# Gram products in rounds of four, logits copied by ScalarE, turned gate factors and four system transfers in a delta-attention and mixture-of-experts kernel

## The chip, the cores and the metric

The kernel runs as one program on one core of a Trainium2 chip. The metric is the device time of one execution in microseconds (us); lower is better. Five engines work side by side, each through its own list of instructions in order: TensorE (PE; its weight loads are listed as PEld), VectorE (DVE), ScalarE (ACT), GpSimd (POOL) and SyncE (SP), which here only issues DMA transfers. ACT and POOL issue some transfers too.

## The reference

All of it is in float32. Three stages follow each other: a delta-rule attention over 4 x 8 heads with a state of 48 x 48 per head, a dense layer with a squared ReLU, and a top-1 mixture of eight experts.

```python
# q, k, v: (4, 8, 768, 48); beta: (4, 8, 768)
k_n = k / (np.linalg.norm(k, axis=-1, keepdims=True) + 1e-06)
for t in range(S):
    y[:, :, t] = np.einsum('bhd,bhde->bhe', q[:, :, t], state)
    v_old = np.einsum('bhde,bhd->bhe', state, kt)
    state = state + bt[:, :, :, None] * np.einsum('bhd,bhe->bhde', kt, vt - v_old)
x = y.transpose(0, 2, 1, 3).reshape(3072, 384)
x = np.maximum(x @ w_in, 0.0) ** 2 @ w_out            # w_in (384, 2048)
logits = x @ w_gate                                    # w_gate (384, 8)
gate_w = softmax(logits)[argmax]                       # one factor per token
out[token] = gate_w * (np.maximum(x @ w1[e], 0) @ w2[e])   # e = argmax, w1 (8, 384, 1024)
```

## The kernel before

**Chunks and units.** The 768 steps of the attention are cut into 12 chunks of 64. For each chunk the dense layer is computed in 8 units: `l1_unit` (18 products `h`, L682) and, two units later, `l2_unit` (12 products `x`, L710). The attention of later chunks is spread between these units as generators. A chunk has 16 half-unit slots, and the tables `PRE2_AT` and `CHAIN_AT` say at which slot a generator makes its next step (`step_bg`). Every engine runs what it gets in this order.

**Preparing a chunk: `pre(c)`.** For c from 4 on it starts two chunks ahead. `front(c)` turns keys and queries on DVE (`kq`, L381, from the loaded tile `st`), and then makes the Gram products of the keys with keys and queries: 32 heads, in four groups (`grams`, L383 to L409) at slots 5, 6, 7 and 8. A group takes 4 times two products `gm` (L392 and L393), each of 48 rows by 64 columns of weights and 128 columns of data, into one PSUM bank. Each product is two passes in the trace, so that a group is 16 records. ACT empties the bank: `gd` (keys with keys), and `kq` for the queries, which POOL then masks (L401). `bounce` writes `gd` to a buffer `dg` in device memory (4 transfers from ACT, slot 8); `bounced` reads it back as `gl`, with one small system in each partition (2 transfers from SP, slot 8.6).

**Solving: `solve`.** From slot 12.3 on DVE solves 64 triangular systems of 32 x 32 per chunk, 31 steps of a product (`tmp`, L520) and a subtraction (`pt`, L525). The first instruction is a square root on ACT (L476) of the diagonal of `gl`. At the end SP writes the result to `dt` (2 transfers, L535) and reads it back in another order as `tt` (8 transfers, L545). `gl` has one buffer, so that the next one can't be loaded before the solve has read the last.

**The chain: `chain(c)`**, in the chunk before c: at slot 7 it loads `ktok` and multiplies `z` (L583); then `u` from `tt` and `vz` (L594, slot 10.6), `z`, `u`, and `y` twice, which make the dense layer's input `xt`; the state is updated by `ku` (L641) at slot 0.1 of the next chunk. All of these small products, the transposes and the logits take turns in four PSUM banks of the pool `ps_a`: the n-th tile gets the bank of the (n-4)-th, and waits until that one is read.

**Routing: `route(c)`**, in the chunk after c: the output rows of the dense layer are written to device memory (`xs_d`, L727), transposed (`xp`, L734) and multiplied by the gate weights (`lp`, L742); DVE copies the logits to `lga` (L743), and finds the expert and the place in its list, which POOL scatters to `list_d` (L793). `gates` (L799) turns the logits into gate factors, and SP writes them to `g_d` token by token: for 10 chunks 4 transfers of 64 x 10 single floats from `ga` (L809).

**Experts.** From the last chunk on: `load_ids` reads a list (SP, L1017), `gather` fetches the rows `xg` from `xs_d` and `gather_gate` the factors `gg` from `g_d` (POOL, L1023 and L1032), `transposed` turns the rows on PE (`xp`, L1045), and `slot` does two products per expert (`h` L1059, `y` L1071). Slots 0 and 1 have 256 rows; slots 2 to 9 up to 384 (L1081, L1091). The weights are loaded as `raw` (SP, 7 transfers of 384 or 512 KB per slot) and split by ACT and DVE into `ew`.

Of the kernel before, what the change touches and what calls it, by code (L numbers as in the profile page):

```python
# [41 lines left out]
def kernel(  # L42
# [19 lines left out]
    P = 128  # L62
# [302 lines left out]
    def front(c):  # L365
# [20 lines left out]
        def grams(hf, g, c0, c1):  # L386
# [9 lines left out]
            for x in range(2):  # L396
# [10 lines left out]
                if c0 == 0 and c1 == P:  # L407
                    nc.scalar.copy(kq[l, x, rs, 32:64], gm[l, :, 32:64])

        masks = []  # L410

# [5 lines left out]
        def bounce():  # L417
            dgv = dg.rearrange("(u r two) s t -> u two s r t", u=2, two=2)
# [28 lines left out]
        else:  # L447
            yield
            transposes(1)
            load_v(c)  # L450
            yield
            for n, hg in enumerate(groups):
                masked()
                grams(*hg, 0, P)
                if n == 3:
                    bounce()
                yield
# [10 lines left out]
    def solve(cs):  # L468
# [28 lines left out]
        def norms(n):  # L497
            c = cs[n]
            nps = ps_a.tile([P, NPR], F32, tag="a", name="nps")
            for x in range(2):  # L500
                for hf in range(2):
                    for u in range(2):
                        r0, l0 = quad(x, hf), 32 * u + 16 * hf
                        nc.tensor.matmul(nps[r0:r0 + 32, HP * u:HP * u + HP], nl[0:64, part[n]], ident[0:64, l0 + x:l0 + 16:2], start=True, stop=True)
# [32 lines left out]
        for c, dt in zip(cs, dts):  # L537
            tt = ap_.tile([P, 2, HP, 32], F32, tag="tt", bufs=2, name=f"tt{c}")
            tt_t[c] = tt
            dtr = dt.rearrange("(u f r two) j t -> f two u j r t", u=2, f=2, two=2)  # L540
            for u in range(2):
                for hf in range(2):
                    for x in range(2):
                        r0 = quad(x, hf)
                        (nc.gpsimd if c == 0 and x else nc.sync).dma_start(out=tt[r0:r0 + 32, u], in_=dtr[hf, x, u])  # L545
            yield
# [14 lines left out]
    def chain(c):  # L561
# [4 lines left out]
        if c + 1 < NCH:  # L566
            ktok = ap_.tile([P, NPR, D], F32, tag="ktok", name=f"ktok{c}")
            load_k(c, ktok)
        if c == 0:
            yield  # L570
# [18 lines left out]
        def u_step(u):  # L589
            ut = ps_a.tile([P, HP, D], F32, tag="a", name="u")  # L590
            for j in range(HP):
                for hf, x in heads:
                    o = quad(x, hf)
                    nc.tensor.matmul(ut[o:o + 32, j], tt[o:o + 32, u, j], vt[o:o + 32, u, j], start=True, stop=True)  # L594
            for hf, x in heads:
# [121 lines left out]
    def route(c):  # L717
# [81 lines left out]
    def gates(c0, c1):  # L799
# [3 lines left out]
        nc.scalar.activation(lf, lf, AF.Exp)  # L803
        nc.vector.tensor_reduce(out=ga, in_=lf, axis=AX.X, op=ALU.add)
        nc.vector.tensor_scalar(ga, ga, 1e-9, None, op0=ALU.add)
        nc.vector.reciprocal(ga, ga)
        gv = ga.rearrange("p (c t) -> p t c", t=2)
# [17 lines left out]
    def load_bl():  # L825
        for par in range(2):
            for u in range(2):
                r0 = 64 * par + 32 * u
                nc.gpsimd.dma_start(out=bl[r0:r0 + 32], in_=bf[:, :, u, :])

# [335 lines left out]
    for n, (c, i) in enumerate(units):  # L1166
# [32 lines left out]
        if c == NCH - 1 and i == 0:  # L1199
            gates(0, NCH - 2)  # L1200
        if c == NCH - 1 and i == 2:
            for n in range(NFS):
                gx[n] = gather(n, ids[n]) + (gather_gate(n, ids[n]),)
        if c == NCH - 1 and i > NF // 2 - 1 - KD:
# [4 lines left out]
    for a in pend:  # L1209
        l2_unit(*a)  # L1210
        split_w(0, j)
        j += 1
    xT_next, todo = transposed(0)
    for t in todo:
        t()
    last = route(NCH - 1)
    advance(last)
    while j < NW:
        split_w(0, j)
        j += 1  # L1220
    tab = slot_table()

    def ahead(s):
# [4 lines left out]
    def slot(s):  # L1228
# [21 lines left out]
        for i in range(NF2 // 2):  # L1250
# [9 lines left out]
            split_w(s + 1, 2 * i)  # L1260
            if s == 0:
                if i == 2:
                    run(last)
                    gates(NCH - 2, NCH)
                    ahead(0)
            turn_one()
# [113 lines left out]
```

## Time and profile before

| | |
|---|---|
| median of 3 runs | 1021.74 us (1018.74 to 1023.69) |
| the profiled execution: its time, its span | 1019.3 us, 1017.5 us |
| busy in the span: PE, DVE, ACT, POOL | 910.4, 664.9, 514.3, 315.4 us |
| mean granted clock of TensorE, as a share of full speed | 0.957 |
| Gram products `gm`: records, first to last | 768, 10.9 to 601.8 us |

The time is 1.8 us longer than the span, from the first to the last instruction in the trace. All later times are counted from the start of the span. The attention with the dense layer goes on until about 711 us, the experts until the end. An engine's busy time says how long something ran on it, not that it set the end; that is read from the waits in each stretch.

### The profile page before, as it was taken

What the parts mean: (1) busy time and instruction counts of PE and PEld (TensorE: products, weight loads), DVE (VectorE), ACT (ScalarE), POOL (GpSimd) and SP (SyncE); (2) the same over time, 40 slices, a digit from 0 to 9 for tenths busy, and PEclk for the clock granted to TensorE, in tenths of its full rate; (3) what the DMA queues carried; (4) which work ended last, traced back from release to release, by engine and by line L of the source; (5) the groups of instructions that cost most, each with busy time, mean ns of one, the idle gap of its engine ahead of it and who ended that gap; (6) DMA issues with size and microseconds to landing.
All of it is one profiled execution on the core that took longest, in us unless ns stands there. A gap on an engine that the chain in (4) does not pass through costs nothing.

```text
span 1017.5 us, 28821 instructions
## 1 busy us (share of the span) xinstructions
PE 910.4 (89%) x11416; PEld 849.9 (84%) x11416; DVE 664.9 (65%) x2270; ACT 514.3 (51%) x1025; POOL 315.4 (31%) x322
## 2 busy tenths in 40 slices
PE   6267979999899999999999999999789999999995
PEld 5135868988898888888888988999779999998994
DVE  6987897584949495868686777424564554463653
ACT  5146755555354645454545555455444444464553
POOL 2020023333142424242424342210434334353231
PEclk9689889999899999999999999999899999999998
DMA  8899292535343443435342531218786555564764
GB/s 159 139 184 272 40 103 31 84 38 85 49 83 50 77 56 57 61 57 74 63 72 49 80 55 38 38 55 140 139 251 209 158 165 174 165 218 136 236 199 133
DMA packets 273021, 113.82 MB, mean 112 GB/s; under 512 B 241053, under 2 KB 259554, under 8 KB 272096
## 3 DMA queue, kind: packets, MB, share of 16 engines
q1 hardware_dynamic: 244176, 92.87, 43.3%
q0 software_dynamic: 7344, 15.17, 5.8%
q10 hardware_dynamic: 21344, 3.67, 2.2%
q8 instruction: 100, 1.64, 0.8%
q14 instruction: 57, 0.47, 0.2%
HBM read 95.01 MB, written 17.82 MB: 111 GB/s over the span
## 4 chain that ended last, share of the span: by engine, by line
PE 54%; DVE 18%; DMA 12%; issue 5%; SPq 5%; ACT 4%; POOL 1%; another core or an unknown queue 0%; ACTq 0%; DVEq 0%; POOLq 0%
PE h L682 12%; PE x L710 11%; PE h L1059 6%; PE y L1071 5%; DVE tmp L520 5%; DVE pt L525 4%; PE h L1081 4%; PE y L1091 3%; DVE kq L381 2%; DMA raw<-in_moe_w_dram 2%; PE gm L392 2%; DMA xs_d<-xr 2%; PE wa L1091 2%; DMA st<-in_q_dram 1%; DMA xg<-xs_d,ids 1%
## 5 line engine op out<-in xcount | busy, mean ns | idle before, releaser
L682 PE MATMUL h<-xt,win 128*128 128x256 f32 x1728 | 235.1, 291 | 6.0 <-issue 2.9
L710 PE MATMUL x<-wout,gt 128*128 128x384 f32 x1152 | 229.1, 347 | 2.7 <-issue 2.3
L682 PEld LDWEIGHTS h<-xt,win 128*128 128x128 f32 x1728 | 220.6, 195 | 12.4 <-issue 5.1
L710 PEld LDWEIGHTS x<-wout,gt 128*128 128x128 f32 x1152 | 200.9, 192 | 9.7 <-issue 6.9
L692 POOL TENSOR_TENSOR gt<-r,gt 128x512 fp32r<-128x512 f32 x80 | 103.7, 1296 | 320.5 <-ACT gt L688 216.5
L520 DVE TENSOR_TENSOR tmp<-pt,gl 128x60 f32<-128x60 f32 (+37 forms) x662 | 142.4, 254 | 1.8
L686 ACT ACTIVATE r<-h 128x512 f32<-128x512 f32 x96 | 57.4, 597 | 166.9 <-PE h L682 118.9
L525 DVE TENSOR_TENSOR pt<-pt,tmp 128x60 f32<-128x60 f32 (+37 forms) x662 | 135.1, 243 | 4.3 <-remote 3.0
L973 DVE TENSOR_TENSOR ew<-raw,ew 128x768 fp32r<-128x768 f32 (+1 forms) x98 | 102.3, 1069 | 9.2 <-ACT ew L972 8.5
L1059 PE MATMUL h<-xgT,ew 128*128 128x256 f32 x648 | 85.0, 287 | 7.5 <-issue 4.5
L1059 PEld LDWEIGHTS h<-xgT,ew 128*128 128x128 f32 x648 | 82.1, 195 | 9.8 <-issue 7.3
L972 ACT CAST ew<-raw 128x768 fp32r<-128x768 f32 (+1 forms) x98 | 87.4, 923 | 1.9 <-DMA raw<-in_moe_w_dram 1.9
L1071 PE MATMUL y<-ew,ht 128*128 128x384 f32 x432 | 86.3, 347 | 0.0
L1071 PEld LDWEIGHTS y<-ew,ht 128*128 128x128 f32 x432 | 75.7, 193 | 0.1
L1101 POOL DMA_INDIRECT out_dram<-yo,ids x30 | 30.2, 1005 | 127.3 <-ACT yo L1100 119.2
L1063 DVE SCALAR_TENSOR_TENSOR ht<-h,ht 128x512 fp32r<-128x512 f32 x36 | 24.8, 690 | 65.9 <-ACT ht L1062 65.8
L1023 POOL DMA_INDIRECT xg<-xs_d,ids x36 | 44.2, 1229 | 71.5 <-DVE ew L973 42.6
L687 ACT ACTIVATE r<-r 128x512 f32<-128x512 f32 x96 | 60.7, 632 | 3.0
L688 ACT CAST gt<-r 128x512 fp32r<-128x512 f32 x96 | 59.6, 620 | 5.0 <-ACT r L687 0.4
L401 POOL TENSOR_TENSOR kq<-kq,qmask 64x256 f32<-64x256 f32 x72 | 53.4, 742 | 23.0 <-ACT kq L400 18.8
L597 ACT COPY sw<-u 32x384 f32<-32x384 f32 x96 | 45.1, 470 | 23.9 <-PE u L594 21.9
L392 PE MATMUL gm<-kq 48*64 48x128 f32 (+1 forms) x384 | 47.3, 266 | 7.1 <-DVE lga L743 5.4
(229 smaller groups left out, 1354.4 us busy)
## 6 DMA issues: line engine op xcount, KB each, us to landing
raw<-in_moe_w_dram SPq DMA_DIRECT2D x45, 512.0 KB
raw<-in_moe_w_dram SPq DMA_DIRECT2D x60, 384.0 KB
gl<-dg SPq DMA_DIRECT2D x24, 256.0 KB
rawo<-in_moe_w_out_dram SPq DMA_DIRECT2D x8, 768.0 KB
xs_d<-xr SPq DMA_DIRECT2D x48, 96.0 KB
ktok<-in_k_dram SPq DMA_DIRECT2D x22, 192.0 KB
dt<-pt SPq DMA_DIRECT2D x24, 128.0 KB
tt<-dt SPq DMA_DIRECT2D x92, 32.0 KB
```

The lines of the kernel that those rows point to most:

```text
L392: nc.tensor.matmul(gm[64:128, j, c0:c1], kq[0:D, 0, r, 0:CH], kq[0:D, 0, r, c0:c1], start=True, stop=True)
L520: nc.vector.tensor_tensor(out=tv, in0=pt[:, js, s:s + 1].to_broadcast([P, m, n]), in1=gl[:, s:s + 1, s + 1:32].to_broadcast([P, m, n]), op ...
L525: nc.vector.tensor_tensor(out=pt[:, js, s + 1:32], in0=pt[:, js, s + 1:32], in1=tv, op=ALU.subtract)
L682: nc.tensor.matmul(h[:, f2], win_t[kk, half][:, wl, f0:f0 + P], xt[:, xl, kk], start=(n == 0), stop=(n == 3 * KD - 1))
L687: nc.scalar.activation(r, r, AF.Square)
L688: nc.scalar.copy(gt[:, 0], r)
L692: eng.tensor_tensor(out=gt[:, 1], in0=r, in1=gt[:, 0], op=ALU.subtract)
L710: nc.tensor.matmul(x2_t[c][t], gt[:, gl_, f2, ts_], wout_t[i][:, wl, f2], start=(f == 0 and n == 0), stop=(f == NF - 1 and n == 2),)
L972: nc.scalar.copy(dst[:, 0], raw)
L973: nc.vector.tensor_tensor(out=dst[:, 1], in0=raw, in1=dst[:, 0], op=ALU.subtract)
L1059: nc.tensor.matmul(h[:, f2], a[kk][:, wl, f * P:f * P + P], xgT[:, xl, kk, 0:SLOT], start=(n == 0), stop=(n == 3 * KD - 1))
L1071: nc.tensor.matmul(y, ht[:, hl, f2, ts_], b[i][:, wl, f2], start=(f == 0 and n == 0), stop=(f == NF2 - 1 and n == 2),)
```

## The change

- `quarters` takes the place of `grams` for c from 3 on, at the first and third Gram step of a chunk. It issues two groups at once, into two PSUM banks, in rounds of four products: rows 0 to 63 and 64 to 127 of the array with each of its two halves of columns. Each of the four steps empties one bank. In the second bank the halves are exchanged, so that `gd` is emptied there in two copies of 64 partitions instead of one of 128.
- The heads stand in another order in `dg` and `dt`, so that `tt` comes in four transfers of 64 KB instead of eight of 32 KB; `beta` is loaded in eight transfers instead of four, on POOL at the start.
- `chain(c)` for c from 3 on loads `ktok` at a step of its own at slot 4.6.
- The logits `lga` are copied by ACT instead of DVE, but for the last chunk; there DVE instead of ACT scales the output rows.
- `gates` transposes the factors on PE, copies them by ACT (`gT`) and writes 10 (at the end 2) contiguous rows of 64 floats per transfer; it is split in two steps. The gathers of the rows for the first three slots are issued ahead of the writing of the factors, and those of the factors behind it. The last `route` starts before the transposes of slot 0.

```diff
+        def quarters(hf, emptied):
+            kq = kqs[hf]
+            gms = [ps_a.tile([P, 4, P], F32, tag="a", name=f"gm{g}") for g in range(2)]
+            for j in range(4):
+                for g, gm in enumerate(gms):
+                    for x in range(2):
+                        k0, o, r = 64 * x, 64 * (1 - x ^ g), 4 * g + j
+                        nc.tensor.matmul(gm[o:o + 64, j], kq[k0:k0 + D, x, r, 0:CH], kq[k0:k0 + D, x, r], start=True, stop=True)
+
+            def empty(g):
+                gm, rs = gms[g], slice(4 * g, 4 * g + 4)
+                r0 = hf * HP + 4 * g
+                if g == 0:
+                    nc.scalar.copy(gd[:, r0:r0 + 4, :], gm[:, :, 0:CH])
+                for x in range(2):
+                    t0, o = 64 * (1 - x), 64 * (1 - x ^ g)
+                    h, l = slice(t0, t0 + 64), slice(t0, t0 + 32)
+                    if g:
+                        nc.scalar.copy(gd[h, r0:r0 + 4, :], gm[o:o + 64, :, 0:CH])
+                    nc.scalar.copy(kq[h, x, rs, CH:P], gm[o:o + 64, :, CH:P])
+                    nc.gpsimd.tensor_tensor(
+                        out=kq[h, x, rs, CH:P], in0=kq[h, x, rs, CH:P],
+                        in1=qmask[h].unsqueeze(1).to_broadcast([64, 4, CH]), op=ALU.mult,
+                    )
+                    nc.scalar.copy(kq[l, x, rs, 32:64], gm[o:o + 32, :, 32:64])
+
+            emptied.extend((lambda: empty(0), lambda: empty(1)))
...
+                if c >= 3:
+                    if n % 2 == 0:
+                        quarters(n // 2, emptied)
+                    emptied.pop(0)()
+                    if n == 3:
+                        bounce()
+                    yield
+                    continue
                 grams(*hg, 0, P)
...
-            for u in range(2):
-                for hf in range(2):
-                    for x in range(2):
-                        r0 = quad(x, hf)
-                        (nc.gpsimd if c == 0 and x else nc.sync).dma_start(out=tt[r0:r0 + 32, u], in_=dtr[hf, x, u])
+            for hf in range(2):
+                for x in range(2):
+                    r0 = quad(x, hf)
+                    (nc.gpsimd if c == 0 and x else nc.sync).dma_start(
+                        out=tt[r0:r0 + 32].rearrange("p r u t -> p (r u) t"), in_=dtr[hf, x],
+                    )
...
-        if c == 0:
+        if c == 0 or c > 2:
             yield
...
-            nc.scalar.activation(xr, x2p[t], AF.Copy, scale=2.0 ** -LIFT)
+            if c == NCH - 1:
+                nc.vector.tensor_scalar(xr, x2p[t], 2.0 ** -LIFT, None, op0=ALU.mult)
+            else:
+                nc.scalar.activation(xr, x2p[t], AF.Copy, scale=2.0 ** -LIFT)
...
-            nc.vector.tensor_copy(lg[:, t], lp)
+            (nc.vector.tensor_copy if fast else nc.scalar.copy)(lg[:, t], lp)
...
+        yield
+        gp = ps_a.tile([n, P], F32, tag="a", name="gp")
+        nc.tensor.transpose(gp, ga, ident)
+        gT = p2.tile([n, P], F32, bufs=1, name=f"gT{c0}")
+        nc.scalar.copy(gT, gp)
...
-                out=g_d[b * S + c0 * CH:b * S + c1 * CH, :].rearrange("(c p) o -> p (c o)", p=CH),
-                in_=gv[64 * (b % 2):64 * (b % 2) + 64, b // 2],
+                out=g_d[b * S + c0 * CH:b * S + c1 * CH, :].rearrange("(c p) o -> c (p o)", p=CH),
+                in_=gT[b // 2 * m:b // 2 * m + m, 64 * (b % 2):64 * (b % 2) + 64],
...
+    CHAIN.update({c: (c - 1, (4.6,) + SCHED["CHAIN_AT"]) for c in range(3, NCH)})
```

PE's list, from the second half of one transposed tile to the `z` of the chain, in a chunk of the middle; before (the repeats of a group's pairs left out):

```order
L734 MATMUL xp<-ident,xr_3878 128x128 x3
L392 MATMUL gm<-kq_132 64x128
L393 MATMUL gm<-kq_132 64x128
...
L682 MATMUL h<-xt_3593,win 128x256 x18
L392 MATMUL gm<-kq_132 64x128
...
L742 MATMUL lp<-wg,x2T 128x8 x3
L734 MATMUL xp<-ident,xr_3882 128x128 x3
L392 MATMUL gm<-kq_133 64x128
...
L583 MATMUL z<-sw,kq_130 32x48 x2
```

The same place with the change (`gm_3966` and `gm_3967` are the two banks of the first call):

```order
L775 MATMUL xp<-ident,xr_3870 128x128 x3
L417 MATMUL gm_3966<-kq_132 64x128 x2
L417 MATMUL gm_3967<-kq_132 64x128 x2
...
L720 MATMUL h<-xt_3585,win 128x256 x18
...
L783 MATMUL lp<-wg,x2T 128x8 x3
L775 MATMUL xp<-ident,xr_3874 128x128 x3
L417 MATMUL gm_4059<-kq_133 64x128 x2
L417 MATMUL gm_4060<-kq_133 64x128 x2
...
L621 MATMUL z<-sw,kq_130 32x48 x2
```

The second and the fourth group have moved up into the first and the third: between the first call and `lp` no Gram product is left, and none stands behind `z`.

SP's list between the stores of output rows and the loads of the next keys, once per chunk, before:

```order
L727 DMA xs_d<-xr_6528 64x384 x2
L535 DMA dt_6662<-pt_6138 1024x1x32 x2
L545 DMA tt_6665<-dt_6662 32x8x32 x8
L284 DMA ktok_6729<-in_k_dram 64x16x48 x2
L430 DMA gl_6823<-dg_6396 64x1024 x2
```

and with the change:

```order
L768 DMA xs_d<-xr_6514 64x384 x2
L284 DMA ktok_6595<-in_k_dram 64x16x48 x2
L572 DMA dt_6660<-pt_6124 1024x1x32 x2
L581 DMA tt_6663<-dt_6660 32x16x32 x4
L458 DMA gl_6807<-dg_6382 64x1024 x2
```

`ktok` has moved ahead of `dt`, and four transfers stand between `dt` and `gl` where there were ten.

POOL's list at the start of the last chunk, before:

```order
L1023 DMA xg_10796<-xs_d,ids_10642 128x384 x2
L1032 DMA gg_10799<-g_d,ids_10642 128x1 x2
L1023 DMA xg_10802<-xs_d,ids_10644 128x384 x2
L1032 DMA gg_10805<-g_d,ids_10644 128x1 x2
L793 DMA list_d<-tid,pos 24960x1 x4
```

and with the change:

```order
L1072 DMA xg_10766<-xs_d,ids_10616 128x384 x2
L1072 DMA xg_10769<-xs_d,ids_10618 128x384 x2
L1081 DMA gg_10828<-g_d,ids_10616 128x1 x2
L1081 DMA gg_10831<-g_d,ids_10618 128x1 x2
L834 DMA list_d<-tid,pos 24960x1 x4
```

The rows of both slots are now fetched before any factor. On SP the four stores to `xs_d` of that time stand ahead of the four to `g_d` where they stood behind, and the list of slot 2 is read ahead of the last four stores to `g_d`.

## Rows read from the trace of the kernel before

**Rows 1.** Timeline of PE, two Gram groups (start us, us, engine, line, operation)

```profile
433.38 0.32 PE L392 MATMUL gm<-kq 48*64 48x128 f32 x1
...
433.54 0.27 PE L392 MATMUL gm<-kq 48*64 48x128 f32 x1
...
434.19 0.27 PE L392 MATMUL gm<-kq 48*64 48x128 f32 x1
...
434.40 2.42 PE L682 MATMUL h<-xt,win 128*128 128x256 f32 x18
...
441.00 0.32 PE L392 MATMUL gm<-kq 48*64 48x128 f32 x1
```

**Rows 2.** Timeline of PE, the state update

```profile
423.51 0.94 PE L641 MATMUL ku<-sw,ktok 64*48 64x48 f32 x64
424.38 2.42 PE L682 MATMUL h<-xt,win 128*128 128x256 f32 x18
```

**Rows 3.** PE's waits: us in total, times, longest

```profile
PE gm L392 <- DVE lga L743: 5.4, 5, 1.3
```

**Rows 4.** Timeline of SP, from one solve to the next

```profile
446.11 1.25 SPq L535 DMA_DIRECT2D dt<-pt  x2
451.23 3.81 SPq L545 DMA_DIRECT2D tt<-dt  x8
455.14 1.35 SPq L284 DMA_DIRECT2D ktok<-in_k_dram  x2
456.60 1.55 SPq L430 DMA_DIRECT2D gl<-dg  x2
```

**Rows 5.** Timeline of ACT: last `dg` transfers and first instruction of the solve

```profile
453.15 1.31 ACTq L422 DMA_DIRECT2D dg<-gd  x2
...
463.12 0.26 ACT L476 ACTIVATE s<-gl 128x32 f32<-128x32 f32 x1 [2.72 <-DMA gl<-dg]
```

**Rows 6.** Timeline of DVE: first and last instruction of that solve

```profile
463.41 0.18 DVE L479 TENSOR_SCALAR s<-s 128x32 f32<-128x32 f32 x1 [2.90 <-ACT s L476]
...
497.80 0.29 DVE L525 TENSOR_TENSOR pt<-pt,tmp 128x8 f32<-128x8 f32 x2
```

**Rows 7.** Engines in one period from solve to solve (length, busy and count each)

```profile
549.87:601.02 51.15, 49.10 (x791) 45.74 (x791) 37.79 (x167) 27.35 (x61) 18.29 (x18) 1.00 0.43 67
```

**Rows 8.** Timeline of ACT: the second Gram group is emptied

```profile
438.73 0.36 ACT L395 COPY gd<-gm 128x256 f32<-128x256 f32 x1
...
439.91 0.25 ACT L408 COPY kq<-gm 32x128 f32<-32x128 f32 x1
```

**Rows 9.** Timeline of SP: factors written in the last chunk, list of slot 2 read

```profile
685.34 7.74 SPq L809 DMA_DIRECT2D g_d<-ga  x4
...
745.80 0.39 SPq L1017 DMA_DIRECT2D ids<-list_d  x1
```

**Rows 10.** Chain that ended last (start us, us, what)

```profile
693.81 15.37 DMA xs_d<-xr
...
753.98 7.24 DMA xg<-xs_d,ids
```

**Rows 11.** Engines in stretches of 5 us (last columns: clock, DMA share, GB/s)

```profile
696.00:701.00 5.00, 5.00 (x40) 4.96 (x40) 3.08 (x11) 2.86 (x5) 0.00 (x0) 1.00 1.05 29
...
761.00:766.00 5.00, 4.74 (x17) 4.64 (x18) 1.12 (x2) 1.54 (x3) 3.31 (x4) 0.50 0.29 100
```

**Rows 12.** Timeline of POOL: first gather

```profile
711.03 0.99 POOL L1023 DMA_INDIRECT xg<-xs_d,ids  x1 [42.59 <-DVE ew L973]
```

**Rows 13.** Timeline of PE: gathered rows for slots 0 and 2

```profile
716.83 1.54 PE L1045 MATMUL xp<-ident,xg 128*128 128x128 f32 x6 [5.49 <-DMA xg<-xs_d,ids]
718.94 4.21 PE L1059 MATMUL h<-xgT,ew 128*128 128x256 f32 x18 [0.57 <-ACT xgT L1047]
...
758.78 0.55 PE L1045 MATMUL xp<-ident,xg 128*128 128x128 f32 x3 [3.18 <-DMA xg<-xs_d,ids]
761.26 0.90 PE L1045 MATMUL xp<-ident,xg 128*128 128x128 f32 x3 [0.73 <-DMA xg<-xs_d,ids]
```

More of the change, by code (lines that the diff above doesn't have):

```diff
@@ L417, in bounce @@
         def bounce():
-            dgv = dg.rearrange("(u r two) s t -> u two s r t", u=2, two=2)
+            dgv = dg.rearrange("(r u two) s t -> u two s r t", u=2, two=2)
             for u in range(2):
@@ L451, in front @@
             yield
+            emptied = []
             for n, hg in enumerate(groups):
                 masked()
+                if c >= 3:
[6 more added lines that the diff above has]
+                    continue
                 grams(*hg, 0, P)
@@ L502, in norms @@
                     for u in range(2):
-                        r0, l0 = quad(x, hf), 32 * u + 16 * hf
-                        nc.tensor.matmul(nps[r0:r0 + 32, HP * u:HP * u + HP], nl[0:64, part[n]], ident[0:64, l0 + x:l0 + 16:2], start=True, stop=True)
+                        r0, l0 = quad(x, hf), 32 * hf + 2 * u + x
+                        nc.tensor.matmul(nps[r0:r0 + 32, HP * u:HP * u + HP], nl[0:64, part[n]], ident[0:64, l0:32 * hf + 32:4], start=True, stop=True)
             ncol = ap_.tile([P, NPR], F32, tag="ncol", bufs=2, name=f"ncol{c}")
@@ L537, in solve @@
         for c, dt in zip(cs, dts):
-            tt = ap_.tile([P, 2, HP, 32], F32, tag="tt", bufs=2, name=f"tt{c}")
+            tt = ap_.tile([P, HP, 2, 32], F32, tag="tt", bufs=2, name=f"tt{c}")
             tt_t[c] = tt
-            dtr = dt.rearrange("(u f r two) j t -> f two u j r t", u=2, f=2, two=2)
-            for u in range(2):
-                for hf in range(2):
-                    for x in range(2):
-                        r0 = quad(x, hf)
-                        (nc.gpsimd if c == 0 and x else nc.sync).dma_start(out=tt[r0:r0 + 32, u], in_=dtr[hf, x, u])
+            dtr = dt.rearrange("(f r two) j t -> f two j r t", f=2, two=2)
+            for hf in range(2):
[4 more added lines that the diff above has]
+                    )
             yield
@@ L593, in u_step @@
                     o = quad(x, hf)
-                    nc.tensor.matmul(ut[o:o + 32, j], tt[o:o + 32, u, j], vt[o:o + 32, u, j], start=True, stop=True)
+                    nc.tensor.matmul(ut[o:o + 32, j], tt[o:o + 32, j, u], vt[o:o + 32, u, j], start=True, stop=True)
             for hf, x in heads:
@@ L803, in gates @@
         nc.scalar.activation(lf, lf, AF.Exp)
-        nc.vector.tensor_reduce(out=ga, in_=lf, axis=AX.X, op=ALU.add)
+        nc.vector.tensor_reduce(out=ga.rearrange("p (t c) -> p c t", t=2), in_=lga[:, c0:c1], axis=AX.X, op=ALU.add)
         nc.vector.tensor_scalar(ga, ga, 1e-9, None, op0=ALU.add)
         nc.vector.reciprocal(ga, ga)
-        gv = ga.rearrange("p (c t) -> p t c", t=2)
+        yield
[3 more added lines that the diff above has]
+        nc.scalar.copy(gT, gp)
+        m = c1 - c0
         for b in range(NB):
             nc.sync.dma_start(
-                out=g_d[b * S + c0 * CH:b * S + c1 * CH, :].rearrange("(c p) o -> p (c o)", p=CH),
-                in_=gv[64 * (b % 2):64 * (b % 2) + 64, b // 2],
+                out=g_d[b * S + c0 * CH:b * S + c1 * CH, :].rearrange("(c p) o -> c (p o)", p=CH),
+                in_=gT[b // 2 * m:b // 2 * m + m, 64 * (b % 2):64 * (b % 2) + 64],
             )
@@ L827, in load_bl @@
             for u in range(2):
-                r0 = 64 * par + 32 * u
-                nc.gpsimd.dma_start(out=bl[r0:r0 + 32], in_=bf[:, :, u, :])
+                for x in range(2):
+                    r0 = 64 * par + 2 * u + x
+                    nc.gpsimd.dma_start(out=bl[r0:64 * par + 64:4], in_=bf[x::2, :, u, :])
     def keep_warm(a, b, n):
@@ L1199 @@
         if c == NCH - 1 and i == 0:
-            gates(0, NCH - 2)
+            ga_steps = gates(0, NCH - 2)
+            advance(ga_steps)
         if c == NCH - 1 and i == 2:
+            gx.update({n: gather(n, ids[n]) for n in range(NFS)})
+        if c == NCH - 1 and i == 3:
+            run(ga_steps)
             for n in range(NFS):
-                gx[n] = gather(n, ids[n]) + (gather_gate(n, ids[n]),)
+                gx[n] += (gather_gate(n, ids[n]),)
         if c == NCH - 1 and i > NF // 2 - 1 - KD:
@@ L1212 @@
         j += 1
+    last = route(NCH - 1)
+    advance(last)
     xT_next, todo = transposed(0)
@@ L1215 @@
         t()
-    last = route(NCH - 1)
     advance(last)
@@ L1221 @@
     tab = slot_table()
+    gb_steps = gates(NCH - 2, NCH)
     def ahead(s):
@@ L1260, in slot @@
             split_w(s + 1, 2 * i)
[L1261 to L1265, printed above, removed]
+            if s == 0 and i == 2:
+                run(last)
+                advance(gb_steps)
+                gx[2] = gather(2, load_ids(2))
+            if s == 0 and i == 3:
+                run(gb_steps)
+                gx[2] += (gather_gate(2, gx[2][0]),)
             turn_one()
```

## Prediction

> **What bounds the kernel now.** I read the engines' busy time by stretches first, to find stretches with one limit each; then PE's waits and its timeline there; and last, where PE waited, the chain of waits and the lists of SP, ACT and DVE.
>
> Between 170 and 640 us the work repeats once per chunk. In the period of [rows 7] PE is busy for 49.10 of 51.15 us, so that PE looks like the limit. But a second loop closes in the same time. The reader is to follow one solve: its first instruction on DVE is at 463.41 and its last ends at 498.09, 34.7 us without a pause [rows 6]. Behind a solve SP writes `dt` (446.11), has to wait until it has landed, issues eight `tt` (from 451.23), two `ktok` and only then `gl` (456.60) [rows 4]. ACT's square root waits for `gl` until 463.12 [rows 5], and the next solve starts. 17.3 us from end to start and 34.7 us of solve make 52.0 us, the length of the period. PE is tied to the loop too: it waits for a Gram bank until DVE, behind the whole solve, has copied the logits, 5.4 us in five waits [rows 3]. So both limits stand within some 3 us of each other, and a gain on one alone is cut off by the other.
>
> At the start of the last chunk and in the first expert slots PE is not the limit. It waits 5.49 us for the rows of slot 0 and 3.18 and 0.73 us for those of slot 2 [rows 13].
>
> **The Gram products.** A group takes 1.02 us (433.38 to 434.40); from its second step to its last the pairs follow at 0.108 us ((434.19 - 433.54) / 6) [rows 1]. A call of `quarters` has 32 records in 8 rounds of four. If a round takes as long as a pair did, a call takes 1.02 us and a chunk saves 2 x 1.02 = 2.04 us; if a round takes as long as two pairs, nothing. The nearest row is the state update, which already runs on the same four quarters: 64 records in 0.87 us, 0.054 us per round of four [rows 2]. At the Gram's rate of 0.108 / 128 us per column its 48 columns need 0.041 us, and two pairs in turn would need 0.081. So four overlap, with at most 0.014 us over their stream. I take 0.108 us, with 0.122 as the other end: 9 chunks x 2.04 = 18.4 us, at least 9 x 1.82 = 16.4, and 0 if the update isn't a measure for wider weights.
>
> [...]
>
> **The logits.** Off DVE, the copy follows the product at once. The bank that it releases is also another one now. All 5.4 us go [rows 3]; 0 to 5.4 are the bounds. ACT pays two copies of some 0.2 us per chunk.
>
> **The new wait.** Two banks are filled at once, and the second is emptied only a step later on ACT, behind the next unit's three activations. The second call needs that bank for its third product. In [rows 8] the emptying at that step starts at 438.73 and ends at 440.16; with one `gd` copy of 0.36 more it ends at about 440.5. PE reaches the place of the second call at 441.00 [rows 1], less the 1.02 us of the group that is gone: 439.98. So PE waits some 0.5 us per chunk, 9 x 0.5 = 4.5 us; bounds are 0 (ACT less late than that) and 9. Behind the waiting product stand the chain's `z` and the next unit. PE's side of the sum is 18.4 + 5.4 - 4.5 = 19.3 us.
>
> **The loop.** It must give way too. `ktok` (1.35 us) leaves the way from `dt` to `gl`. Four `tt` of 64 KB are issued instead of eight in 3.81 us: between 1.9 us (half of it) and 2.5 us (as `dt`, 0.62 us each for 128 KB) [rows 4]. From 451.23 on, `gl` could go at 453.3 instead of 456.60. It also waits for `dg`. The last two of its transfers left ACT at 453.15 and took until 454.46 [rows 5], because before them stood the wait for a solve's end (by the logits and the fourth group) and for the transfers of `tt`, whose counters they share. With the change the Gram call is a slot earlier and the last `dg` has only `dt` ahead of it. So I put `gl` at 454.0, 2.6 us earlier; between 1.3 (only `ktok` gained) and 3.3. The period falls from 52.0 to 49.4 us. PE alone would need 51.15 - 1.0 (logits) - 2.04 + 0.5 = 48.6 us. The loop is the longer by a little, so that I take 2.1 us per chunk, 9 x 2.1 = 19 us for the attention, with 10 and 24 as the ends.
>
> **Rows for slot 0.** Four stores of single floats to `g_d` are issued from 685.34 for 7.74 us [rows 9], and the stores to `xs_d` behind them land 15.37 us after 693.81 [rows 10]. From 696 to 701 the DMA engines were busy all the time and moved 29 GB/s [rows 11]: the floats hold them. POOL's gather could go only at 711.03 [rows 12]. With the change `xs_d` is ahead of `g_d`, and the factors are 10 rows of 256 bytes per transfer. The gather needs 5.8 us from its issue to PE's start; it has to go by 705, and the stores can now go out from 685. PE saves 5.49 us, and 1.8 us of a slow start: its 18 products at 718.94 took 4.21 us, 2.42 in [rows 1]. Against that, DVE has two scaling copies ahead of the turned rows, 0.5 us that show. 5.5 + 1.8 - 0.5 = 6.8 us; bounds 3 and 8.
>
> **Rows for slot 2.** Its list was read at 745.80 [rows 9], behind the second writing of factors, and its rows landed 7.24 us after 753.98 [rows 10]. [...] The list now goes ahead of the factors, but the rows compete with the weight loads as before. [...]
>
> **What costs nothing.** Four more loads of `beta` on POOL lie ahead of a long pause of that engine (if not, under 3 us). Two transposes of factors on PE are 0.6 us. ACT's 0.7 us more per chunk have 51.15 - 27.35 us of free time to lie in [rows 7]; what shows of them is the wait above.
>
> **The sum.** 19 + 6.8 + 3 = 28.8 us off the profiled execution's 1019.3 us gives 990.5. That execution is 2.4 us under the median of the runs, 1021.74; I add 1.5 us for that and forecast 992 us.
>
> **The rivals.** *The loop holds.* `gl` goes only 1.3 us earlier, as `dg` or the landing of `tt` is late, and 9 x 1.0 us remain of the attention's 19: 1002 us. For it speaks that [rows 5] show `dg` going out last before `gl`; against it that two reasons of that lateness are removed. *No overlap.* Rounds take two pairs' time: 5.4 us remain of the attention (the new wait is within the longer call): 992 + 13.6 = about 1005 us. The update's row speaks against it. *The rows are late all the same.* 3 MB of weights are ahead of `xs_d` in SP's queue: 992 + 9.8 = 1002 us. Against it speaks that the weights were through before 696, when almost nothing moved. *Slower: ACT is late with the second bank.* The wait of 0.5 us grows, as ACT's emptying comes behind activations that wait for POOL and PE. At 3.7 us per chunk, 28.8 / 9 + 0.5, the gain is eaten; at 5 us the time is 992 + 9 x 4.5 = 1032 us. [rows 8] show ACT in time by over 3 us, so that it needs a second delay. [...]
>
> **How the numbers follow.** The forecast has a chance of 0.62, with 984 to 998 as its own range (the ends of the loop and of slot 0). The loop that holds has 0.18, late rows 0.08, no overlap 0.07, slower 0.05. The range goes from 983 to 1006: it takes in the first four cases up to their times, and leaves out the slower one and mixtures below and above. 0.5% of 1021.74, 5.1 us, is about what a measurement of this kernel tells from no change. Of the chances, 0.93 are faster by more than that, 0.03 within it (a mixture of two of the rivals, or a mild delay of ACT), 0.04 slower.
>
> **What would show it.** Right: Gram calls of about 1.0 to 1.1 us, two per chunk; no wait of PE for `lga`; a short wait of the second call for ACT; `gl` some 8 us behind `dt` instead of 10.5; periods of 49 to 50 us; the first gather before 705 us less what was gained by then, and no clock of 0.50 there. Wrong: rounds above 0.13 us, `gl` still 10 us behind `dt`, or PE waiting over 2 us for ACT's emptying or for `tt` ahead of `u`.

## The result, and the profile after

The changed kernel takes 1008.75 us (median of 4 runs, 1002.9 to 1018.54) against 1020.24 us; the ratio is 0.9847, with an interval from 0.9802 to 0.9892. It is faster, as forecast, but by less. By the ratio it is 15.6 us, about half of the forecast's 29.7, which puts it at 1004.6 us, inside the range; by the medians it is 11.5 us, and the median lies 2.75 us above the range. The profiled execution is the longest of the four, 1018.5 us, a slow one that the ratio leaves out; what is read from it below stands in the two later traces of the same kernel too (`again`, `again2`), except where said.

The sum of the stretches shows where the time went. In this trace and in the one of before (us from the start of the span; the first and last square root of the steady part are ACT's instructions that open a solve):

| | before | changed | difference |
|---|---|---|---|
| first such square root | 136.01 | 140.66 | +4.7 |
| from there to the last one | 480.1 | 488.0 | +7.9 |
| from there to the last product `x` of the dense layer | 95.3 | 96.8 | +1.6 |
| from there to the end (the experts) | 306.2 | 291.3 | -14.9 |

So in this trace the experts gained more than forecast (9.8), and the attention, for which 19 us were forecast, gained nothing. Neither size is to be taken from these two executions alone. The second row is not longer in the later traces: `again` has 473.3 us there, beside 474.3 in `end_only`, which has the attention of before on the same chip. And `attn_only`, with the experts' part of before, takes 300.5 us in the last row, 5.7 less than before's own trace. The Gram calls themselves did what they should. Timeline of PE in a chunk of the middle, both Gram calls:

```profile
445.46 1.10 PE L417 MATMUL gm<-kq 48*64 48x128 f32 x32
446.50 2.42 PE L720 MATMUL h<-xt,win 128*128 128x256 f32 x18
...
451.88 0.43 PE L417 MATMUL gm<-kq 48*64 48x128 f32 x4
452.60 1.09 PE L417 MATMUL gm<-kq 48*64 48x128 f32 x28 [0.29 <-ACT kq L434]
453.62 0.48 PE L621 MATMUL z<-sw,kq 48*32 48x48 f32 x25
```

The first call takes 1.04 us from its start to the next unit, the second 1.74 with its wait for ACT's emptying. Four groups of 1.02 us [rows 1] have become 2.78: 1.3 us saved per chunk. PE's waits from 170 to 660 us (us in total, times, longest) tell what became of that:

```profile
PE u L632 <- DMA tt<-dt: 7.6, 13, 1.1
PE x L748 <- issue: 6.3, 1, 6.3
...
PE gm L417 <- ACT kq L434: 2.6, 9, 0.3
...
PE u L632 <- ACT lga L784: 1.9, 2, 1.0
PE u L632 <- ACT gt L726: 0.9, 1, 0.9
```

The wait for `lga` [rows 3] is gone from the Grams. In its place PE waits at the product `u` for the solved systems `tt`, and for ACT. The reader is to follow one solve to the next. SP's timeline behind the solve that ends at 458.15:

```profile
458.18 1.25 SPq L572 DMA_DIRECT2D dt<-pt  x2
462.49 1.94 SPq L581 DMA_DIRECT2D tt<-dt  x4
464.99 1.13 SPq L458 DMA_DIRECT2D gl<-dg  x2
```

`gl` goes 6.8 us behind `dt`; it was 10.5 [rows 4]. But the square root no longer waits for it (it has no wait in ACT's timeline; of the nine steady ones of this trace one still waits for `gl`, 0.4 us), it stands behind the cast of a dense unit:

```profile
472.38 0.62 ACT L726 CAST gt<-r 128x512 fp32r<-128x512 f32 x1
472.91 0.25 ACT L513 ACTIVATE s<-gl 128x32 f32<-128x32 f32 x1
```

That unit is the one behind `u` in PE's timeline:

```profile
464.85 0.24 PE L632 MATMUL u<-vz,tt 32*32 32x48 f32 x2 [0.96 <-ACT lga L784]
465.50 0.61 PE L632 MATMUL u<-vz,tt 32*32 32x48 f32 x4 [0.41 <-DMA tt<-dt]
466.33 0.87 PE L632 MATMUL u<-vz,tt 32*32 32x48 f32 x58 [0.23 <-DMA tt<-dt]
467.13 3.86 PE L720 MATMUL h<-xt,win 128*128 128x256 f32 x18
```

Its 18 products take 3.86 us where they take 2.42 elsewhere. The stretches (length, then busy time and count of PE, PEld, DVE, ACT and POOL, then clock, DMA share, GB/s) show the clock beside it: PE stood idle for half of the first, and the granted clock was 0.67 over the second, at 0.50, the lower of the two levels in the trace, for 3.41 us from 467.00 on.

```profile
463.00:466.00 3.00, 1.55 (x12) 0.96 (x10) 1.10 (x2) 1.77 (x4) 1.10 (x1) 1.00 0.70 112
466.00:469.00 3.00, 2.77 (x68) 2.60 (x67) 1.33 (x9) 1.67 (x4) 0.16 (x1) 0.67 0.93 204
```

The solve itself has grown too. Its first instruction on DVE starts with POOL's product of the same dense unit, and ends with it (timelines of POOL and of DVE, and all of DVE's in one line: shortest, middle and longest in ns):

```profile
473.08 1.28 POOL L730 TENSOR_TENSOR gt<-r,gt 128x512 fp32r<-128x512 f32 x1 [6.92 <-ACT gt L726]
```

```profile
473.19 1.21 DVE L516 TENSOR_SCALAR s<-s 128x32 f32<-128x32 f32 x1
```

```profile
L516 DVE TENSOR_SCALAR s<-s x11: 195/1207/1214, 27.6 to 629.0; 128x32 f32<-128x32 f32 x10, 128x64 f32<-128x64 f32 x1
```

It was 0.18 us in [rows 6]. So the periods from square root to square root are 51 to 53 us long, with a mean clock of 0.97 (first and last of four stretches; [rows 7] have 51.15 and 1.00):

```profile
420.53:472.91 52.38, 48.99 (x792) 45.87 (x792) 41.09 (x164) 27.56 (x65) 17.87 (x18) 0.97 0.47 69
...
577.59:628.64 51.05, 48.95 (x792) 45.81 (x792) 39.84 (x163) 27.54 (x65) 18.16 (x18) 0.97 0.38 60
```

At the last chunk, POOL's first gather goes 16 us ahead of the end of the dense layer (725.47), and PE finds its rows (the gather's line names a landing of `g_d` as what ended its wait; it reads `xs_d`, issued just before, and which landing it was isn't settled); SP's stores to `xs_d` stand ahead of those to `g_d`, which take 3.75 us instead of 7.74 [rows 9, 12, 13]. Timelines of SP, POOL and PE:

```profile
699.31 4.10 SPq L768 DMA_DIRECT2D xs_d<-xr  x4
704.00 3.75 SPq L855 DMA_DIRECT2D g_d<-gT  x4
```

```profile
709.48 0.99 POOL L1072 DMA_INDIRECT xg<-xs_d,ids  x1 [26.52 <-DMA g_d<-gT]
```

```profile
725.31 0.82 PE L1094 MATMUL xp<-ident,xg 128*128 128x128 f32 x6
725.96 0.82 PE L775 MATMUL xp<-ident,xr 128*128 128x128 f32 x6
726.75 0.39 PE L1108 MATMUL h<-xgT,ew 128*128 128x256 f32 x1
727.42 2.25 PE L1108 MATMUL h<-xgT,ew 128*128 128x256 f32 x17 [0.29 <-DVE xgT L1097]
```

### The profile page after: what moved, and what is told of

Read it like the earlier page. It is cut to its first block, busy times and chain, and to the rows that moved or that the text cites. A ratio compares the mean times of both kernels' runs of the same rounds, so it can differ in the third digit from the quotient of the medians.

```text
span 1016.8 us, 28824 instructions
## 1 busy us (share of the span) xinstructions
PE 903.3 (89%) x11418; PEld 845.5 (83%) x11418; DVE 684.1 (67%) x2250; ACT 519.6 (51%) x1065; POOL 317.2 (31%) x324
## 4 chain that ended last, share of the span: by engine, by line
PE 53%; DVE 19%; DMA 12%; issue 6%; ACT 4%; SPq 3%; POOL 1%; ACTq 0%; DVEq 0%; POOLq 0%
PE h L720 12%; PE x L748 11%; PE h L1108 7%; DVE tmp L557 6%; PE y L1120 6%; DVE pt L562 5%; PE h L1130 4%; PE y L1140 3%; DMA dt<-pt 2%; DVE kq L381 2%; PE u L632 2%; PE wa L1140 2%; DMA st<-in_q_dram 2%; DMA vz<-in_v_dram 2%; DMA rawi<-in_moe_w_in_dram 1%
## 5 line engine op out<-in xcount | busy, mean ns | idle before, releaser
L720 PE MATMUL h<-xt,win 128*128 128x256 f32 x1728 | 238.7, 294 | 8.3 <-issue 7.5
L720 PEld LDWEIGHTS h<-xt,win 128*128 128x128 f32 x1728 | 224.7, 199 | 14.0 <-issue 9.7
L748 PEld LDWEIGHTS x<-wout,gt 128*128 128x128 f32 x1152 | 203.5, 194 | 11.9 <-issue 8.1
L557 DVE TENSOR_TENSOR tmp<-pt,gl 128x60 f32<-128x60 f32 (+37 forms) x662 | 149.1, 263 | 3.9 <-remote 2.0
L1120 PE MATMUL y<-ew,ht 128*128 128x384 f32 x432 | 83.9, 340 | 0.0
L1120 PEld LDWEIGHTS y<-ew,ht 128*128 128x128 f32 x432 | 73.6, 188 | 0.1
L430 POOL TENSOR_TENSOR kq<-kq,qmask 64x256 f32<-64x256 f32 x72 | 53.1, 738 | 16.8 <-ACT kq L429 12.7
L381 DVE STREAM_TRANSPOSE kq<-st 64x512 f32<-64x512 f32 x72 | 50.8, 706 | 1.2
```

The lines of the kernel that those rows point to most:

```text
L381: nc.vector.transpose(out=kqs[hf][r, x, :, i * CH:(i + 1) * CH].rearrange("p r (u t) -> p r u t", u=2), in_=st[i][r, hf * HP:(hf + 1) * HP],)
L557: nc.vector.tensor_tensor(out=tv, in0=pt[:, js, s:s + 1].to_broadcast([P, m, n]), in1=gl[:, s:s + 1, s + 1:32].to_broadcast([P, m, n]), op ...
L720: nc.tensor.matmul(h[:, f2], win_t[kk, half][:, wl, f0:f0 + P], xt[:, xl, kk], start=(n == 0), stop=(n == 3 * KD - 1))
L748: nc.tensor.matmul(x2_t[c][t], gt[:, gl_, f2, ts_], wout_t[i][:, wl, f2], start=(f == 0 and n == 0), stop=(f == NF - 1 and n == 2),)
L1120: nc.tensor.matmul(y, ht[:, hl, f2, ts_], b[i][:, wl, f2], start=(f == 0 and n == 0), stop=(f == NF2 - 1 and n == 2),)
```

## The experiments

The cases ran on three chips, A, B and C, with the kernel before beside them: 1007.3 us on A, 1019.7 on B, 1007.2 on C. So ratios are compared, and medians only on one chip. "First root", "steady" and "rest" are rows one, two and four of the table above, for the one profiled execution of each.

| run | median us | ratio to before | first root | steady | rest |
|---|---|---|---|---|---|
| `again` (chip A) | 998.35 | 0.9908 (0.9873 to 0.9942) | 139.2 | 473.3 | 289.3 |
| `no_quarters` | 995.80 | 0.9896 (0.9865 to 0.9928) | 139.8 | 472.7 | 288.5 |
| `u_later` | 1003.69 | 0.9964 (0.9936 to 0.9993) | 141.5 | 468.6 | 288.1 |
| `end_only` | 996.12 | 0.9903 (0.9873 to 0.9933) | 136.3 | 474.3 | 289.6 |
| `warm` (chip B) | 1017.15 | 0.9961 (0.9926 to 0.9996) | 142.3 | 480.3 | 296.9 |
| `no_T` | 998.15 | 0.9786 (0.9744 to 0.9827) | 135.8 | 479.1 | 291.2 |
| `attn_only` | 1018.88 | 0.9975 (0.9942 to 1.0008) | 140.3 | 476.0 | 300.5 |
| `factors_only` | 1013.10 | 0.9930 (0.9901 to 0.9959) | 136.3 | 479.0 | 295.9 |
| `again2` (chip C) | 998.96 | 0.9914 (0.9883 to 0.9946) | 141.6 | 474.7 | 292.7 |
| `no_T2` | 993.50 | 0.9876 (0.9835 to 0.9918) | 136.4 | 468.8 | 288.2 |
| `bl_after` | 997.56 | 0.9907 (0.9883 to 0.9932) | 137.8 | 478.9 | 294.2 |
| `no_T_Q` | 996.34 | 0.9875 (0.9832 to 0.9919) | 135.6 | 472.2 | 290.5 |

The steady part of one profiled execution varies by more than the cases differ: 473.3, 474.7 and 488.0 us for the changed kernel, on three chips. It can't rank them; the ratios and the waits can.

**`again`: the changed kernel, unedited.**

> The changed kernel once more, nothing edited, for a second trace beside the one of 1018.5 us, in which the attention ended 14 us later than before and the experts took 15 us less. Theory A (TensorE is now early at the first product u of a chunk, waits some 2 us for tt, and its clock then halves for some 3.4 us in nearly every chunk): the same half-clock stretches stand in this trace, some 8 of them between 200 and 640 us, and the time is 1003 to 1010 us, as the start-up before 170 us varies. Theory B (that execution was an accident): no stretches at u, the attention ends before 705 us, time under 1003 us.

This chip is 1.3% faster by the kernel before, so that the time alone tells nothing; the ratio is 0.991, no better than the 0.985 of the result. The waits at `u` are there in this trace too (PE's waits between 400 and 612 us), though the lower clock shows in six places between 200 and 640 us, where the first trace has nine; three of the six lie behind `u`. Theory B falls.

```profile
PE u L632 <- DMA tt<-dt: 5.2, 8, 0.9
PE gm L417 <- ACT kq L434: 1.2, 4, 0.3
```

**`no_quarters`: the four groups of before, the rest of the change kept.** The edit takes `quarters` and its branch in `front` out again:

```diff
-                if c >= 3:
-                    if n % 2 == 0:
-                        quarters(n // 2, emptied)
-                    emptied.pop(0)()
-                    ...
                 grams(*hg, 0, P)
```

> Grams made in four groups as before, all other parts of the change kept. Theory A (the loop solve, dt, tt, u, square root, solve sets the period; what TensorE saves is spent idle at u and at half clock): TensorE is some 2 us per chunk busier, waits less at u, and the half-clock stretches go: the time stays within 4 us of the changed kernel's, or is less. Theory of the prediction (TensorE's work is the path): 9 x 2.04 less 4.5 = 14 us slower than the changed kernel.

2.5 us less than `again`, where the prediction's way of thinking gives 14 more. PE has more to do and waits less for `tt` in the same stretch (the lower clock shows in two places between 200 and 640 us, neither of them behind `u`):

```profile
PE u L595 <- DMA tt<-dt: 1.0, 4, 0.5
```

**`u_later`: the chain from `u` on half a unit later.**

```diff
-    CHAIN.update({c: (c - 1, (4.6,) + SCHED["CHAIN_AT"]) for c in range(3, NCH)})
+    CHAIN.update({c: (c - 1, (4.6, 7, 11.4, 12.6, 13.6, 14.5, 14.6)) for c in range(3, NCH)})
```

> The changed kernel with the steps of the chain from the first u on put one half unit later, so that TensorE does one more unit before it needs tt. Theory A: the wait at u and the half-clock stretches go, the solve starts as soon as gl lands (some 12.8 us behind the last one's end, not 14.7), the period falls by about 2 us: 9 x 2 = 12 to 20 us faster than the changed kernel. Rival (the period is TensorE's work, or the later y holds up the next chunk's first unit): within 4 us, with new waits of h for xt.

The wait for `tt` went, and the square root came 12.1 to 12.4 us behind a solve in three of the later periods. But the time is not less, it is 5 us more than that of `again`. The second `u` of the chunk now waits for `vz`, whose subtraction stands behind the start of the solve on DVE, and the unit behind it runs at the lower clock, 3.92 us for its 12 products, which take 2.25 us in the first trace at 448.75, at full clock (PE's timeline):

```profile
460.94 0.88 PE L632 MATMUL u<-vz,tt 32*32 32x48 f32 x64 [1.86 <-DVE vz L625]
461.75 3.92 PE L748 MATMUL x<-wout,gt 128*128 128x384 f32 x12
```

Each of the two engines waits for the other once per chunk; moving a step moves the wait. The solve, begun earlier, also took longer: 38.3 to 39.8 us in the last four full periods, where that of `again` took 36.4 to 37.9. My expectation failed: the period did not fall.

**`end_only`: the kernel before with the parts at the last chunk and the first slots alone** (the hunks of `gates`, the gathers, the last `route` and the scaling by DVE).

> The kernel before with only the parts of the change at the last chunk and the first expert slots (turned factors, order of the gathers, last route early, output rows scaled by VectorE there). If the two parts of the program don't touch, the 14.8 us that the experts gained in the trace are all there: 1005 us against 1020 before, and the attention's part of the change is worth nothing or less. The prediction gave these parts 9.8 us: 1010 us. If the gain hung on the attention's state: under 5 us.

0.9903, as much as the whole change on that chip (0.9908): 9.8 us of 1007.3, by medians 11.2. PE's only waits from 640 to 800 us:

```profile
PE x L710 <- issue: 0.3, 1, 0.3
PE h L1068 <- DVE xgT L1057: 0.3, 1, 0.3
PE xp L1054 <- DMA xg<-xs_d,ids: 0.2, 1, 0.2
```

**`warm`: twelve products ahead of the first `u`.**

```diff
             ut = ps_a.tile([P, HP, D], F32, tag="a", name="u")
+            if c > 2 and u == 0:
+                for _ in range(12):
+                    nc.tensor.matmul(ut.rearrange("p a b -> p (a b)")[:, 0:P], ident, ident, start=True, stop=True)
```

> The changed kernel with twelve products of 128 x 128 that nobody reads ahead of the first u of a chunk, in the bank of u, some 2 us of work for TensorE in the place where it waits for tt. The output stays what it was. Theory A (the wait for tt, and the half clock behind it, give back what the rounds of four save): the half-clock stretches behind u go, the unit behind u takes 2.4 us, not 3.3 to 3.9, the period falls from 51.2 by 1 to 1.5 us, in all 8 to 12 us faster than the changed kernel. Rival (the period is set elsewhere, in VectorE's solve and its way back, whatever TensorE does): the clock is full and the time within 3 us of the changed kernel's.

In the place it did what theory A says. The timeline of PE has no wait and a full clock (each product is two records, and the first line holds the second half of the twelve), and the two last full periods took 50.0 us on average (in `again`, on another chip, 51.3; in `attn_only`, on this one, 50.9):

```profile
565.79 1.50 PE L631 MATMUL u<-ident 128*128 128x128 f32 x12
567.22 0.88 PE L635 MATMUL u<-vz,tt 32*32 32x48 f32 x64
568.03 2.42 PE L723 MATMUL h<-xt,win 128*128 128x256 f32 x18
```

```profile
522.47:572.37 49.90, 49.56 (x817) 47.01 (x816) 40.00 (x164) 27.52 (x66) 18.22 (x18) 1.00 0.43 68
572.37:622.52 50.15, 49.82 (x817) 47.24 (x816) 40.24 (x164) 27.52 (x65) 18.18 (x18) 1.00 0.40 62
```

The time did not follow: 0.9961, not better than the changed kernel's 0.991. Three other periods of this trace took 54 to 57 us, and its rest is 3 to 9 us longer than in the other cases with all parts at the end; there PE waits up to 4 us at a time for nothing that the profile shows. Whether the added products cause that isn't known. The changed kernel itself was not run on this chip.

**`no_T` and `no_T2`: the old order of heads**, with eight `tt` and four loads of `beta` (the hunks of `bounce`, `norms`, `tt`, `u_step` and `load_bl` undone).

> The changed kernel with the old order of heads in dg and dt, that is eight transfers tt instead of four, and beta in four transfers instead of eight. If the four more loads of beta ahead of the weights cost the start (the last square root of the start was at 139 to 141 us with them and at 136 us without): that square root is at 136 us again, and the time 3 us less than the changed kernel's, less what the eight tt cost (gl 2 us later behind a solve). If the start varies by itself: 139 us or more here too, and the time within 2 us or slower.

> The changed kernel with the old order of heads (eight tt, four loads of beta) once more, now beside the changed kernel on one chip. If the new order costs the start and no more: last square root of the start at 136 us again, and 3 to 6 us faster than the changed kernel; if the 0.979 of the last call was an accident of that call: the same as the changed kernel.

The first root is back at 136 us in both traces. By medians on chip C, the kernel takes 5.5 us less than the changed kernel; the ratios to before are 0.9876 and 0.9914, whose intervals overlap. On chip B it is 0.9786. On both chips no kernel has a better median, and it is faster than the kernel before beyond doubt; that it is faster than the changed kernel is likely, not shown.

**`attn_only`: all but the parts at the end.**

> The counterpart of the run that had only the parts at the end: all parts of the change in the attention (rounds of four, four tt, early ktok, logits by ScalarE), and the end as before. By the runs so far the attention's parts are worth -2 to 2 us together: within 3 us of the kernel before. By the prediction: 19 us faster.

0.9975, that is 2.5 us of 1019.7, between -0.8 and 5.9 by the interval, where the prediction gives 19. The lost start is in it. PE waits at `u` here too, but in the last three full periods the clock stays full behind the wait, and they take 51.5, 50.3 and 51.5 us; the middle one (PE's timeline, and the engines in that period):

```profile
558.19 0.24 PE L632 MATMUL u<-vz,tt 32*32 32x48 f32 x2 [0.87 <-DMA tt<-dt]
559.05 1.52 PE L632 MATMUL u<-vz,tt 32*32 32x48 f32 x62 [0.62 <-DMA tt<-dt]
```

```profile
514.49:564.83 50.34, 48.19 (x793) 44.85 (x792) 40.66 (x164) 27.60 (x66) 18.17 (x18) 1.00 0.42 68
```

**`factors_only`: the turned factors alone**, the gathers in the old order, each slot's factors behind its rows.

> The kernel before with the turned factors alone: contiguous rows to g_d, but written ahead of the output rows of that time, and the gathers in the old order, each slot's factors behind its rows. If it is the single floats that held the transfers (prediction), this alone gives back most of the wait for slot 0: the first rows leave POOL some 5 us earlier, 4 to 8 us faster than before. If the order on SP and POOL is what counts: under 3 us, and the first gather is as late as before.

7.1 us of 1019.7 (0.9930). POOL's first gather goes 17.6 us ahead of the end of the dense layer (711.6), with `g_d` still ahead of `xs_d`; in the kernel before it went at its end. So it was the single floats that held the stores: SP issued the four transfers in 7.74 us with them [rows 9], in 3.60 us as rows. Timelines of SP and POOL:

```profile
683.39 3.60 SPq L814 DMA_DIRECT2D g_d<-gT  x4
687.77 3.54 SPq L727 DMA_DIRECT2D xs_d<-xr  x4
```

```profile
694.03 1.21 POOL L1029 DMA_INDIRECT xg<-xs_d,ids  x1 [26.52 <-PE x L710]
```

The rows of slot 2 come in time here as well, though their list is still read behind the second writing of factors: PE's waits from 700 to 760 us have none for `xg`, where the kernel before waits 3.18 and 0.73 us [rows 13]. But PE waits 3.6 us for the second factors, which the full change avoids by its two steps:

```profile
PE gp L809 <- DVE ga L806: 3.6, 1, 3.6
```

**`again2`: the changed kernel on chip C.**

> The changed kernel, unedited, beside the three variants of the same call, for their ratios and for one more trace of its start and of TensorE's waits that no semaphore explains (issue), 11 and 19 us of them between 170 and 660 us in the two traces so far. If these waits, longest behind the small products of a chunk, are what spreads its times (990 to 1001 us on one chip), they are another number again, at the same products. Expected ratio to before 0.985 to 0.991.

0.9914. PE's waits without a releaser are 13.7 us in this trace, at the same products.

**`bl_after`: the eight loads of `beta` behind the first weights.** One letter changes place in the order of the start:

```diff
-    ramp="KkqMBLAPAPWaAPWWaaaaSCLipl...",
+    ramp="KkqMLBAPAPWaAPWWaaaaSCLipl...",
```

> The changed kernel with the eight loads of beta behind the first loads of weights on POOL, not ahead of them. If the longer loading of beta in front of the weights is what delays the start by 3 to 5 us: the last square root of the start is at 136 us, and the time 3 to 5 us less than the changed kernel's. If it is the other transfers of the new order (dg, dt, tt), or nothing of both: 139 us or later, and the changed kernel's time.

The first root is at 137.8 us: between the two. The time is 1.4 us less than that of `again2`, less than can be told. By this one trace `beta` ahead of the weights is part of the lost start, and not all of it.

**`no_T_Q`: old order of heads and four groups.**

> Old order of heads and Grams in four groups: of the attention's parts only the early ktok and the logits by ScalarE are left, with all parts at the end. Theory A (what TensorE saves with the rounds of four it waits elsewhere): within 3 us of the run with the old order of heads and rounds of four. Prediction: 14 us slower than it.

2.8 us more than `no_T2`, with the same ratio (0.9875 and 0.9876). Together with `no_quarters` (2.5 us less than `again`) the rounds of four are worth 0, give or take some 4 us, not 14.

## Why the prediction was half right

**The Grams: right in PE's time.** A first call takes 1.04 us, where 1.02 to 1.13 were predicted, so rounds of four overlap: two groups in turn took 2 x 1.02 us [rows 1]. With the wait, the saving is 1.3 us per chunk instead of 2.04 less 0.5.

**The logits and the new wait: right in place and sign.** The 5.4 us are gone, and the second call waits 9 times 0.3 us for ACT (predicted 0.5). But 2.8 us came back as waits of `u` for ACT (3.0 in `again`, 1.8 in `again2`).

**The loop: `gl` right, the conclusion wrong.** `gl` at 6.8 us behind `dt` is earlier than the 8 predicted. The step that failed is "The period falls from 52.0 to 49.4 us" (the last two full ones of `again` take 51.3), and with it "I take 2.1 us per chunk, 9 x 2.1 = 19 us for the attention". The 52.0 us themselves joined the way to one square root with the solve behind it; the two periods that these belong to are 53.1 and 50.3 us long, and the nine of before 53.3 on average. I closed the loop through `gl` and the square root, and there it had been closed: [rows 5] show that wait. I did not look for the next thing that holds the square root: its place in ACT's order, behind a dense unit that stands behind `u`, which waits for `tt`. The prediction named a wait at `u` as what would make it wrong, and that came. Before, PE was tied to the end of the solve by the bank of `lga`; the tie was not cut but moved to `u`. Over the last three full periods the square root came 0.7 us earlier behind a solve (14.9 us instead of 15.5), and the solve took 1.6 us more (37.0 instead of 35.4), 0.9 of them in the one instruction that ends with POOL's product. On chip A it is much the same: 14.2 us in `again` against 15.3 in `end_only`, and 37.0 against 35.4. What is left of PE's saving is idle time at `u`, in most of these periods followed by up to 1.4 us for the lower clock. That the rounds of four gain nothing is shown by two pairs of runs. That the wait and the lower clock behind it cost a period some 1.2 us is suggested by the two clean periods of `warm`, and not shown: they are set against another chip, and beside `attn_only`, which has the wait without the lower clock, they are 0.9 us shorter. That a kernel without both is faster was not shown, as `u_later` and `warm` failed.

**What should cost nothing: wrong.** Four more loads of `beta` were held to be hidden ("if not, under 3 us"). The start is 4.7 us longer in the first pair of traces: 139.2 to 142.3 us in the seven traces with the new order of heads and the old place of `beta`, 135.6 to 136.4 in the six with the old order. How it falls on `beta` and on the other transfers of the new order isn't settled.

**Slot 0: right in kind.** 6.8 us were predicted, with 8 as the upper end. In the two traces PE comes from the end of the dense layer to slot 0's transposes 5.7 us sooner, and from there to those of slot 1 2.5 us sooner, 8.2 in all. The 7.1 us of `factors_only` are another sum: against before's trace it gains the 5.7 too, loses 3.2 in slot 0 by the wait for the second factors, and gains 7.8 around slot 2. The first gather was to go before 705 less what was gained; it went 16 us ahead of the dense layer's end instead of at it.

**Slot 2: too small, and for another reason.** The prediction's sum has 3 us, a term that no run shows. In the two traces the rows gained more: from the transposes of slot 1 to those of slot 2 it was 22.6 us and is 18.5, and 19.3 instead of 22.0 from there to those of slot 3: 6.9 us. The prediction put it down to the place of the list ahead of the factors; `factors_only` gains as much with the list behind them, so that, by this one trace, the single floats held these rows too. The whole of the experts takes 14.9 us less in the first pair of traces. By its ratio, `end_only` gains 9.8 us, on another chip. That this is just the predicted sum of both is partly luck, as in the traces both terms are larger than predicted.

**The sum.** 28.8 us were predicted. The 19 for the attention measure 2.5, with the 4.7 us of the start lost in them, and the 9.8 for the end measure 9.8 by the ratio of `end_only` and 14.9 in the first pair of traces. Of the rivals, "the loop holds" (1002 us) came nearest in its name, by another mechanism: `gl` was early, and the loop held all the same. "No overlap" (about 1005 us) is nearer in time, but the Gram calls of 1.04 us rule it out. ACT was not late with the second bank.

## What to carry to other kernels

Where one engine is busy 96% and a loop through other engines closes in the same time, follow the loop past the wait that ends last: ask what stands next in the order of the engine that waits, and what that depends on. The faster engine waited here at the next thing that it needs (7.6 us at `u` for `tt`), and in several periods TensorE paid for the wait a second time with its lower clock (18 products in 3.86 us instead of 2.42). Single floats to device memory cost more here than their bytes: the same bytes took SP 7.74 us as floats and 3.60 us as rows, and POOL's gather, queued behind them, left 17.6 us ahead of the end of the dense layer instead of at it (`factors_only`). Turning them into rows was the best part of the change, 7.1 us.

## What the runs showed of the hardware that was not expected

A small instruction of DVE (0.18 us) that started 0.1 us behind a POOL product took 1.21 us, until that one ended, in six of the nine steady solves of the changed kernel's trace; in the other three it took 0.72 to 1.16 us, and ended with POOL's product too. So did it once in the trace of before, with 1.20 us at 192.49. The traces show that the two end together, not why.

In every trace PE waits for something that the profile doesn't show ("issue"), 4 to 23 us between 170 and 660 us, mostly behind the many small products of a chunk, and in most traces once for 4 to 7.5 us between 360 and 380 us; the changed kernel's waits above have one of 6.3 us, those of `no_T2` in the same stretch three with 8.3:

```profile
PE x L747 <- issue: 8.3, 3, 6.1
```

That is of the size by which the times of one kernel spread. One guess is the loading of instructions, of which the page of the changed kernel counts (packets, MB, share of the DMA engines' time):

```profile
q8 instruction: 100, 1.64, 0.8%
```

That is 16.4 KB per packet. No run here tells whether these waits are such loads.
